# Scans with a constant of their own, small operations on other engines, and a fixed order of the score matmuls

## The chip, the cores and the metric

The kernel runs on one core of one Trainium2 chip. The metric is the time of one execution in device microseconds, as the median of several runs. In the profile PE is TensorE (PEld its weight loads), DVE is VectorE, ACT is ScalarE, POOL is GpSimd and SP is SyncE, which here only issues DMAs.

## The reference

Three layers follow each other. The first is a gated linear attention over 4 batches, 8 heads, 768 steps and 48 dimensions:

```
for t in range(S):
    state = alpha[t][:, None] * state + outer(k[t], v[t])
    y[t] = q[t] @ state
```

Its output, 3072 tokens by 384, is normalised (RMS) and goes through a gated layer, `silu(x @ w_gate) * (x @ w_val) @ w_out`, with an inner width of 1536. The last layer is a mixture of 8 experts: each token goes to the expert with the largest logit, `relu(x @ w1[e]) @ w2[e]` (inner width 1024), and the result is scaled by two gates. All is float32.

## The kernel before

The attention is cut into 24 tiles of 128 steps (6 per batch). Three tiles make a group of 384 tokens, and there are 8 groups. Tiles 0 to 2 are the first tiles of three batches; in the order of tiles a state is therefore needed again three tiles later.

For one tile, the decay `alpha` is transposed (`al`, 128 partitions by 4 pairs of heads by 128 steps). For tiles 0 to 4 PE transposes it and the scans read PSUM; for tiles 5 and 6 PE transposes and ACT copies to SBUF; from tile 7 on DVE transposes from SBUF. `after_scan` (L310) then runs a scan backwards over the steps: it keeps the first column of `al` in `en`, sets that column to 0, sets the columns `begin[:, 1:, 0]` to 1, scans with `begin` as the added operand and multiplies `en` by the first column of the result, which gives the decay of the state over the whole tile. `upto_scan` (L324) writes reciprocals into `begin[:, :, 0]` and scans forwards with the same `begin`. `k` is multiplied with the one scan and `q` with the other (L351, L411).

`stages` (L415) holds what is done with a tile: `score` multiplies keys by queries on PE (L430), 8 matmuls for 4 pairs of heads and two halves `hh` (partitions 0 to 47 and 64 to 111), into one PSUM bank for each half; each float32 matmul is two records in the trace. Its `post` decays the state by `en` (L434, DVE) and masks the two score banks (L440, DVE). `outp` forms the outputs (L464, L468), whose sum of squares goes through two small POOL operations (L475, L476); `state` adds the tile's own part to the state; `xtr` transposes the result into `xh` and `xl`, the high and low float32r parts.

The gated layer needs weights in two float32r parts as well. They are made while it runs: DVE puts the words of a chunk together (L576, L579, L582), ACT rounds the high part (L595, L622), and DVE subtracts for the low part (L586). For a step j, PE computes `ps_g` and `ps_v` in 9 matmuls each (L650) and `ps_o` in 9 (L684); ACT and DVE turn the first two into `hh` and `hl` (L642, L661, L664, L670). `runs` gives the order: group 0 and group 1 with the steps 0 to 5, then both with the steps 6 to 11, then groups 2 to 7. `m_evac` (L689) copies the three `ps_o` banks after each run. While the first four runs go on, the tiles 3 to 8 of the attention are worked in between; from group 2 on, `strict` fixes the order of PE's instructions as written.

Tokens are scattered by expert into a table in DRAM (`route_b`, POOL's indirect DMAs, L769), which is first filled from a constant row, `zrow`, by way of the tile `zero` (L1010, SP's DMAs, L774). The experts follow, and behind them a branch (`overflow`, L1378) for tokens beyond the slots.

Each engine has one queue and works in order. What order that is, a planner decides when the kernel is built: it simulates the engines and issues on each the instruction that is ready, by order of writing among several. `tc.keep_in_program_order` ties an instruction behind the one written just before it on its engine; `pace` (L223) does so for the kinds listed for a stage, `seq` (L215) where `strict` is set.

```
seq(nc.tensor.matmul(ps[hh][:, p, :], lhsT=kT[r, p, :], rhs=qT[r, p, :], start=True, stop=True))
```

Of the kernel before, what the change touches and what calls it, by code (L numbers as in the profile page):

```python
# [8 lines left out]
F32 = mybir.dt.float32  # L9
# [3 lines left out]
AF = mybir.ActivationFunctionType  # L13
ALU = mybir.AluOpType
# [41 lines left out]
def gla_glu_moe_kernel(  # L56
# [16 lines left out]
    nc = tc.nc  # L73
    P = 128
    B, H, S, D = q.shape
    NT, DM = out.shape
    NP = H // 2
# [8 lines left out]
    GT = 3  # L86
# [4 lines left out]
    RW = DM + 2  # L91
# [7 lines left out]
    FAR = float(1 << 20)  # L99

    const = ctx.enter_context(tc.tile_pool(name="const", bufs=1, side="right"))
# [9 lines left out]
                            base=0, pattern=[[-1, P]], channel_multiplier=1)  # L111
# [3 lines left out]
                            base=0, pattern=[[1, P]], channel_multiplier=-1)  # L115
# [8 lines left out]
                   allow_small_or_imprecise_dtypes=True)  # L124
    tokid = const.tile([P, NTILE, 1], F32, name="tokid")
    nc.gpsimd.iota(tokid[:, 0:NTILE - NCH, 0], pattern=[[P, NCH], [S, B - 1]], base=0, channel_multiplier=1,
                   allow_small_or_imprecise_dtypes=True)
    nc.gpsimd.iota(tokid[:, NTILE - NCH:, 0], pattern=[[P, NCH]], base=S * (B - 1), channel_multiplier=1,
                   allow_small_or_imprecise_dtypes=True)
# [6 lines left out]
                   allow_small_or_imprecise_dtypes=True)  # L136
    rank_at = const.tile([P, E, 1], F32, name="rank_at")
    for r0_, a0_, a1_ in RANKS:
        nc.gpsimd.iota(rank_at[:, a0_:a1_, 0], pattern=[[1, a1_ - a0_]], base=r0_, channel_multiplier=0,
                       allow_small_or_imprecise_dtypes=True)  # L140
# [4 lines left out]
    for i, c in enumerate((REG, DM, F2)):  # L145
# [1 line left out]
    capE = const.tile([P, E, 1], F32, name="capE")  # L147
    gT = const.tile([P, KD], F32, name="gT")
    wr = const.tile([P, KD, RX], F32, name="wr")
    zrow = const.tile([P, 1, RW], F32, name="zrow")  # L150
    nc.gpsimd.memset(zrow, 0.0)
    nc.gpsimd.iota(zrow[:, 0, RW - 1:RW], pattern=[[0, 1]], base=int(FAR), channel_multiplier=1,
                   allow_small_or_imprecise_dtypes=True)


    wpool = tc.alloc_tile_pool(name="wpool", bufs=1, side="left")
# [1 line left out]
    att = tc.alloc_tile_pool(name="att", bufs=1, side="right")  # L158
# [40 lines left out]
    for i in range(1):  # L199
        t_ = att.tile([P, NP, 2 * D], F32, name=f"wide{i}")  # L200
        nc.gpsimd.memset(t_, 0.0)
        wide.append(t_)

    begin = att.tile([P, NP, P], F32, name="begin")
    nc.gpsimd.memset(begin, 0.0)

    vt = {}
    pre = {}
# [4 lines left out]
    strict = [False]  # L213

    def seq(ins):  # L215

        if strict[0]:
            tc.keep_in_program_order(ins)
# [4 lines left out]
    def pace(kind, ins):  # L223

        if kind in paced[0] or kind.rstrip('0123456789') in paced[0]:
            tc.keep_in_program_order(ins)
# [4 lines left out]
    def bank(shape, name):  # L231

        seat[0] += 1
        k_ = SEATS[seat[0] - 1] if spread[0] and seat[0] <= len(SEATS) else seat[0] % 7
        if spread[0] and k_ >= 3:
            return psM.tile(shape, F32, tag=("g", "v", "o0", "o1", "o2")[k_ - 3], name=name)
        return psA.tile(shape, F32, tag="att", name=name)
# [53 lines left out]
    def seat_of(t, nm, shape, bufs=1):  # L291
        if (t, nm) in SIDE:
            tag, i = SIDE[t, nm]
            if tag not in side:
                side[tag] = wpool.tile([P, 3, NP * P], F32, tag=tag, name="side")
            flat = side[tag][:, i, 0:shape[1] * (shape[2] if len(shape) > 2 else 1)]
            return flat.rearrange("p (a b) -> p a b", a=shape[1]) if len(shape) > 2 else flat
        return att.tile(shape, F32, tag=nm, name=nm, bufs=bufs)
# [8 lines left out]
    def flat(x):  # L307
        return x.rearrange("p a b -> p (a b)")

    def after_scan(Z, al):  # L310

        en = att.tile([P, NP, 1], F32, tag="en", name="en", bufs=4)
        W = NP * P
        k_ = 'sc' + str(now[0])
        pace(k_, nc.vector.tensor_copy(en, al[:, :, 0:1]))
        pace(k_, nc.vector.memset(al[:, :, 0:1], 0.0))
        pace(k_, nc.vector.memset(begin[:, 1:, 0:1], 1.0))
        pace(k_, nc.vector.tensor_tensor_scan(out=flat(Z)[:, W - 2::-1], data0=flat(al)[:, W - 1:0:-1],
                                              data1=flat(begin)[:, W - 1:0:-1], initial=1.0,
                                              op0=ALU.mult, op1=ALU.add))  # L320
        pace(k_, nc.vector.tensor_tensor(out=en, in0=en, in1=Z[:, :, 0:1], op=ALU.mult))
        return en

    def upto_scan(A, Z, al):  # L324
# [90 lines left out]
    def stages(t):  # L415
        b, c = place_of[t]
        first, final = c == 0, c == NCH - 1
        en, qT, kT = pre[t]
# [6 lines left out]
        def score():  # L425
            ps = [bank([P, NP, P], "ps_s") for _ in range(2)]
            for p in range(NP):
                for hh in range(2):
                    r = slice(64 * hh, 64 * hh + D)
                    seq(nc.tensor.matmul(ps[hh][:, p, :], lhsT=kT[r, p, :], rhs=qT[r, p, :], start=True, stop=True))  # L430

            def post():
                if not first:
                    nc.vector.tensor_tensor(out=Sc, in0=Sc, in1=en.to_broadcast([P, NP, D]), op=ALU.mult)  # L434
                    for hh in range(2):
                        nc.scalar.activation(S_[rs[hh], :, hh * D:hh * D + D], Sc[rs[hh]], AF.Copy)
                mb = mask.to_broadcast([P, NP, P])
                for hh in range(2):
                    Ph = seat_of(t, f"P{hh}", [P, NP, P])
                    pace(f'Ph{t}', nc.vector.tensor_tensor(out=Ph, in0=ps[hh], in1=mb, op=ALU.mult))  # L440
                    Pt[hh] = Ph
            return post
# [246 lines left out]
    def m_evac(s):  # L689
        g, j0, _ = runs[s]  # L690
        if not j0:
            rows[g] = act.tile([P, GT, WO], F32, tag="R", name="R")
        R = rows[g]
        for i in range(GT):
            if j0:
                nc.vector.tensor_tensor(out=R[:, i, :], in0=R[:, i, :], in1=obank[s][i], op=ALU.add)
            elif i == 1:
                nc.vector.tensor_copy(R[:, i, :], obank[s][i])
            else:
                nc.scalar.activation(R[:, i, :], obank[s][i], AF.Copy)  # L700
        del obank[s]
# [99 lines left out]
    def late_step():  # L801

        if late:
            job = late[0]
            got = job.pop(0)(*carry)
            carry[:] = [] if got is None else [got]
            if not job:
                late.pop(0)
                nconv[1] += 1
# [9 lines left out]
    def prep_step():  # L819
        if prep:  # L820
            prep.pop(0)()

    def slot(s, n):

        g, j0, _ = runs[s]
        j, what = j0 + n // 3, n % 3
        if what == 0:
            have(3 * j + 1, 0)
            return m_gate(g, j)
        if what == 1:  # L830
            have(3 * j + 2, 0)
            return m_val(g, j)
        m_low(g, j)
        if j > j0:
            have(3 * j, j)
            m_out(s, j - 1)
        elif s:
            have(3 * runs[s - 1][2], runs[s - 1][2])
            m_out(s - 1, runs[s - 1][2] - 1)
            return lambda: m_evac(s - 1)  # L840
# [27 lines left out]
    for do in START.split():  # L868
        what, t = do[0], int(do[1:] or 0)
# [108 lines left out]
    for s in range(4):  # L978
        strict[0] = s >= CFG['STRICT']
        N = 3 * (runs[s][2] - runs[s][1])  # L980
        paced[0] = CFG['K2'] if s else CFG['K1']
        for n in range(N):
            if (s, n) == (1, CFG['PREP6']):
                prep.extend(prework(nprep))
                nprep += 1
            late_step()
            post = slot(s, n)
            post2 = []
            while due(s, n):
                post2.append(stage())  # L990
                if s:
                    break
            for i in range(CFG['CR'][s]):
                conv_step()
                if i < CFG['PRN'][s]:
                    prep_step()
                if i == 1 and post:
                    post()
                    post = None
            if post:  # L1000
                post()
            for x in post2:
                if x:
                    x()
            if s == 0 and done % NST == 0:
                while prep:
                    prep_step()
            if s == 3 and n == 0:
                zero = act.tile([P, 1, RW], F32, tag="cF", name="zero", bufs=3)
                nc.scalar.activation(zero, zrow, AF.Copy)  # L1010
            if s == 3 and n < 2 * E and n % 2 == 0:
                init_bucket(n // 2)

# [364 lines left out]
    def overflow():  # L1378
        xp.release()
        op_ = tc.alloc_tile_pool(name="op", bufs=1, side="right", reuse_waits="tile")  # L1380
        with tc.If(nblk > 0):
            with tc.For_i(0, nblk, 1):
                def sm(nm, w=1, dt=F32):
                    return op_.tile([P, w], dt, tag=nm, name=nm)
# [57 lines left out]
                for j in range(KF2):  # L1442
                    ph = psE.tile([P, P], F32, tag="h", name="ph", bufs=2)
                    for i in range(KD):
                        nc.tensor.matmul(ph, lhsT=wa[:, i, j * P:j * P + P], rhs=xo[:, i, :],
                                         start=(i == 0), stop=(i == KD - 1))
# [46 lines left out]
    for u in range(U):  # L1493
        for j in range(KF2):
# [28 lines left out]
            if u > 1 and j == 3:  # L1523
                _, _, r, n = parts[u]
# [22 lines left out]
        if u == 1:  # L1547
            while ready or pw:
                weight_step()
            load_next(2)  # L1550
            fetch()
    op_ = overflow()
    u = U - 1
    for i in range(parts[u][3]):
# [40 lines left out]
```

## Time and profile before

| | |
|---|---|
| median of 3 runs | 820.66 us (820.44 to 821.23) |
| the profiled execution | 820.86 us, of which the span 819.0 us |
| busy, share of the span | PE 98%, PEld 94%, DVE 69%, ACT 40%, POOL 11% |
| granted TensorE clock | 0.997 over the span |

A busy time is the union of an engine's instructions. A matmul's record lasts longer than the time after which the next may start, so a busy PE can still lose time; that is read from the starts of matmuls that follow each other. In a timeline row, `x8` is a merged run of 8 instructions, and the second number is the time from the first's start to the last's end.

### The profile page before, as it was taken

The page shows a single profiled execution, that of the slowest core. Times are in us where ns is not written, and L with a number is a line of the kernel's source. Part 1 is how long each engine was busy: PE and PEld are TensorE (multiplying, and loading weights), DVE is VectorE, ACT ScalarE, POOL GpSimd, SP SyncE. Part 2 cuts the span into 40 slices and gives each one's busy share as a digit, 9 for nine tenths or more (in the row PEclk, how much of TensorE's full clock was granted, in tenths as well). Part 3 has the DMA queues.
Part 4 walks back from the last instruction along what each step waited for, and adds up shares of the span by engine and source line. Part 5 has one row for each costly group of instructions (what it writes and reads, how often), then busy time and mean ns, then how long its engine had stood idle before and what let it go on. Part 6 is the DMA issues. An engine that isn't in the chain of part 4 may idle for free.

```text
span 819.0 us, 15897 instructions
## 1 busy us (share of the span) xinstructions
PE 802.6 (98%) x5967; PEld 771.7 (94%) x5967; DVE 561.4 (69%) x1234; ACT 326.5 (40%) x694; POOL 91.3 (11%) x175
## 2 busy tenths in 40 slices
PE   7999999999999999999999999999999999999996
PEld 5899999999999999999999999999988999999996
DVE  7998999498677876767767662345358667677641
ACT  1756554333333333332433332225226455554441
POOL 3001000000300020010020011010021002211121
PEclk9999999999999999999999999999999999999998
DMA  9955575753543453344444221005047686688710
GB/s 200 215 142 153 160 163 167 214 142 95 146 111 92 113 130 76 83 112 96 102 115 102 47 46 44 20 21 183 1 142 209 169 223 186 214 245 251 204 54 28
DMA packets 195454, 106.85 MB, mean 130 GB/s; under 512 B 125868, under 2 KB 190122, under 8 KB 195376
## 3 DMA queue, kind: packets, MB, share of 16 engines
q1 hardware_dynamic: 190912, 96.35, 46.2%
q0 software_dynamic: 4464, 9.48, 3.5%
q8 instruction: 47, 0.77, 0.4%
q14 instruction: 31, 0.25, 0.1%
HBM read 80.88 MB, written 25.18 MB: 129 GB/s over the span
## 4 chain that ended last, share of the span: by engine, by line
PE 93%; issue 2%; DVE 2%; POOL 1%; ACT 1%; DMA 0%; POOLq 0%; DVEq 0%
PE ps_o L684 19%; PE ps_v L650 19%; PE ps_g L650 19%; PE ps_h L650 12%; PE ps_b L1205 8%; PE ps_s L430 3%; PE ps_b L1211 3%; PE ps_y L468 3%; PE ps_y L464 2%; PE ps_st L489 1%; PE pc L615 1%; PE ps_k L450 1%; PE ps_n L283 1%; DMA er<-bucket 0%; PE pt L607 0%
## 5 line engine op out<-in xcount | busy, mean ns | idle before, releaser
L664 ACT ACTIVATE hh<-tt 128x384 fp32r<-128x384 f32 x96 | 50.3, 524 | 143.2 <-DVE tt L661 133.2
L661 DVE TENSOR_TENSOR tt<-tt,ps_v 128x384 f32<-128x384 f32 x96 | 52.7, 549 | 77.8 <-PE ps_v L650 65.7
L642 ACT ACTIVATE tt<-ps_g 128x384 f32<-128x384 f32 x96 | 47.0, 490 | 86.1 <-PE ps_g L650 80.3
L670 DVE TENSOR_TENSOR hl<-tt,hh 128x384 fp32r<-128x384 f32 x96 | 52.9, 551 | 24.6 <-ACT hh L664 23.0
L1185 DVE SCALAR_TENSOR_TENSOR h<-ps_h,h 128x256 fp32r<-128x256 f32 (+6 forms) x72 | 38.1, 531 | 45.2 <-ACT h L1184 42.5
L684 PE MATMUL ps_o<-wol,hh 128*128 128x400 f32 x192 | 66.3, 346 | 0.0
L684 PE MATMUL ps_o<-woh,hh 128*128 128x400 f32 x192 | 65.2, 348 | 0.0
L1184 ACT ACTIVATE h<-ps_h 128x256 fp32r<-128x256 f32 (+6 forms) x72 | 33.5, 468 | 77.4 <-PE ps_h L650 76.5
L684 PE MATMUL ps_o<-woh,hl 128*128 128x400 f32 x192 | 63.7, 344 | 0.0
L650 PE MATMUL ps_h<-x,w1b 128*128 128x456 f32 (+3 forms) x288 | 57.2, 341 | 0.3 <-DVE h L1185 0.3
L650 PEld LDWEIGHTS ps_h<-x,w1b 128*128 128x128 f32 x288 | 50.6, 188 | 1.9 <-DVE h L1185 0.6
L650 PE MATMUL ps_h<-x,w1a 128*128 128x256 f32 (+3 forms) x288 | 52.2, 325 | 0.0
L650 PEld LDWEIGHTS ps_h<-x,w1a 128*128 128x128 f32 x288 | 47.3, 188 | 0.9 <-ACT x L1165 0.3
L650 PE MATMUL ps_g<-xh,wgh 128*128 128x384 f32 x192 | 46.1, 348 | 0.0
L440 DVE TENSOR_TENSOR P<-ps_s,mask 128x512 f32<-128x512 f32 x46 | 30.1, 685 | 23.0 <-PE ps_s L430 22.8
L650 PE MATMUL ps_v<-xh,wvh 128*128 128x384 f32 x192 | 45.8, 346 | 0.0
L650 PE MATMUL ps_v<-xl,wvh 128*128 128x384 f32 x192 | 44.1, 337 | 0.0
L1205 PE MATMUL ps_b<-h,w2b 128*128 128x456 f32 (+2 forms) x216 | 43.5, 343 | 0.5 <-issue 0.5
L650 PE MATMUL ps_g<-xh,wgl 128*128 128x384 f32 x192 | 44.0, 336 | 0.0
L650 PE MATMUL ps_g<-xl,wgh 128*128 128x384 f32 x192 | 43.8, 337 | 0.0
L650 PE MATMUL ps_v<-xh,wvl 128*128 128x384 f32 x192 | 43.8, 336 | 0.0
L1205 PEld LDWEIGHTS ps_b<-h,w2b 128*128 128x128 f32 x216 | 37.9, 188 | 2.2 <-issue 0.9
(312 smaller groups left out, 1880.3 us busy)
## 6 DMA issues: line engine op xcount, KB each, us to landing
st<-in_moe_w_dram SPq DMA_DIRECT2D x46, 384.0 KB
bucket<-zero SPq DMA_DIRECT2D x8, 772.0 KB
stg<-in_moe_w_gate_dram SPq DMA_DIRECT2D x12, 384.0 KB
stg<-in_moe_w_val_dram SPq DMA_DIRECT2D x12, 384.0 KB
stg<-in_moe_w_out_dram SPq DMA_DIRECT2D x12, 384.0 KB
v<-in_v_dram SPq DMA_DIRECT2D x23, 192.0 KB
more<-in_moe_w_dram SPq DMA_DIRECT2D x9, 384.0 KB
er<-in_moe_w_dram SPq DMA_DIRECT2D x9, 384.0 KB
```

Of the source, the lines that this page charges most:

```text
L430: seq(nc.tensor.matmul(ps[hh][:, p, :], lhsT=kT[r, p, :], rhs=qT[r, p, :], start=True, stop=True))
L440: pace(f'Ph{t}', nc.vector.tensor_tensor(out=Ph, in0=ps[hh], in1=mb, op=ALU.mult))
L468: seq(nc.tensor.matmul(ps[u, h * D:h * D + D], lhsT=Pt[h % 2][:, h // 2, u], rhs=vt[t][:, h, :], start=first, stop=True, skip_group_check= ...
L642: nc.scalar.activation(tt, ps, AF.Silu)
L650: seq(nc.tensor.matmul(ps, lhsT=a_[:, kc, :], rhs=b_[:, kc, :], start=(n == 0), stop=(n == 3 * KD - 1)))
L661: nc.vector.tensor_tensor(out=tt, in0=tt, in1=ps, op=ALU.mult)
L664: nc.scalar.activation(hh, tt, AF.Copy)
L670: nc.vector.tensor_tensor(out=hl, in0=tt, in1=f(hh), op=ALU.subtract)
L684: seq(nc.tensor.matmul(obank[s][i], lhsT=a_[:, sl], rhs=weight(b_, j), start=(j == j0 and n == 0), stop=(j == j1 - 1 and n == 2)))
L1184: nc.scalar.activation(hh[:, 0, :], ps, AF.Relu)
L1185: nc.vector.scalar_tensor_tensor(out=hh[:, 1, :], in0=ps, scalar=0.0, in1=f(hh[:, 0, :]), op0=ALU.max, op1=ALU.subtract)
L1205: nc.tensor.matmul(ob2[u][k_][:, 0:r * n], lhsT=we[p][b_][:, j, k_ * P:k_ * P + P], rhs=hh[:, a_, :], start=(j == 0 and m == 0), stop=(j = ...
```

## The change

The reverse scan gets a constant of its own, `ends` (0, with 1 in the first column of pairs 1 to 3), set once on POOL; the memset of `begin[:, 1:, 0:1]` before each reverse scan is gone. In `after_scan` the copy of `al`'s first column into `en` goes from DVE to ACT, and the product of `en` and `Z` from DVE to POOL; neither is paced any longer. In `score`, for tiles after tile 3, each matmul but the first of a tile is tied behind the one written before it, so that the two halves alternate (`strict` has all of them tied, as before). In `m_evac` the copy of the middle bank goes to ACT for the runs 0 and 1. The constant row `zrow` is no longer kept from the start: POOL writes `zero` itself, and the overflow branch makes its own.

```diff
-    zrow = const.tile([P, 1, RW], F32, name="zrow")
-    nc.gpsimd.memset(zrow, 0.0)
-    nc.gpsimd.iota(zrow[:, 0, RW - 1:RW], pattern=[[0, 1]], base=int(FAR), channel_multiplier=1,
-                   allow_small_or_imprecise_dtypes=True)
+
+    def empty(row):
+        nc.gpsimd.memset(row, 0.0)
+        nc.gpsimd.iota(row[:, 0, RW - 1:RW], pattern=[[0, 1]], base=int(FAR), channel_multiplier=1,
+                       allow_small_or_imprecise_dtypes=True)
...
-    begin = att.tile([P, NP, P], F32, name="begin")
-    nc.gpsimd.memset(begin, 0.0)
+    begin, ends = (att.tile([P, NP, P], F32, name=nm) for nm in ("begin", "ends"))
+    for t_ in (begin, ends):
+        nc.gpsimd.memset(t_, 0.0)
+    nc.gpsimd.memset(ends[:, 1:, 0:1], 1.0)
...
-        pace(k_, nc.vector.tensor_copy(en, al[:, :, 0:1]))
+        nc.scalar.activation(en, al[:, :, 0:1], AF.Copy)
         pace(k_, nc.vector.memset(al[:, :, 0:1], 0.0))
-        pace(k_, nc.vector.memset(begin[:, 1:, 0:1], 1.0))
         pace(k_, nc.vector.tensor_tensor_scan(out=flat(Z)[:, W - 2::-1], data0=flat(al)[:, W - 1:0:-1],
-                                              data1=flat(begin)[:, W - 1:0:-1], initial=1.0,
+                                              data1=flat(ends)[:, W - 1:0:-1], initial=1.0,
                                               op0=ALU.mult, op1=ALU.add))
-        pace(k_, nc.vector.tensor_tensor(out=en, in0=en, in1=Z[:, :, 0:1], op=ALU.mult))
+        nc.gpsimd.tensor_tensor(out=en, in0=en, in1=Z[:, :, 0:1], op=ALU.mult)
...
-                    seq(nc.tensor.matmul(ps[hh][:, p, :], lhsT=kT[r, p, :], rhs=qT[r, p, :], start=True, stop=True))
+                    ins = nc.tensor.matmul(ps[hh][:, p, :], lhsT=kT[r, p, :], rhs=qT[r, p, :], start=True, stop=True)
+                    if strict[0] or (t > GT and (p or hh)):
+                        tc.keep_in_program_order(ins)
...
-            elif i == 1:
+            elif i == 1 and s > 1:
                 nc.vector.tensor_copy(R[:, i, :], obank[s][i])
...
-                nc.scalar.activation(zero, zrow, AF.Copy)
+                empty(zero)
...
+        zrow = op_.tile([P, 1, RW], F32, name="zrow")
         with tc.If(nblk > 0):
+            empty(zrow)
```

## Rows read from the trace of the kernel before

**Rows 1.** The page's chain of work that ended last, by engine.

```profile
PE 93%; issue 2%; DVE 2%; POOL 1%; ACT 1%; DMA 0%; POOLq 0%; DVEq 0%
```

**Rows 2.** Waits of PE: line waited for, us in total, times, longest.

```profile
PE ps_n L283 <- POOL nat L270: 4.4, 1, 4.4
```

**Rows 3.** Stretches: length, busy us (instructions) of PE, PEld, DVE, ACT, POOL; clock, DMA.

```profile
5.00:20.00 15.00, 13.96 (x121) 10.49 (x119) 14.23 (x33) 1.28 (x4) 2.18 (x13) 1.00 1.31 227
...
35.00:50.00 15.00, 15.00 (x143) 14.48 (x142) 15.00 (x37) 7.73 (x16) 0.74 (x2) 1.00 0.58 169
50.00:75.00 25.00, 25.00 (x252) 22.75 (x250) 22.58 (x51) 14.48 (x36) 1.15 (x3) 1.00 0.59 156
```

**Rows 4.** Timeline of PE around tile 4's score matmuls: start, us, instruction.

```profile
51.47 1.16 PE L430 MATMUL ps_s<-qT,kT 48*128 48x128 f32 x8
52.55 0.78 PE L650 MATMUL ps_g<-xh,wgh 128*128 128x384 f32 x3
...
54.31 1.16 PE L430 MATMUL ps_s<-qT,kT 48*128 48x128 f32 x8
55.40 0.81 PE L684 MATMUL ps_o<-woh,hh 128*128 128x400 f32 x3
```

**Rows 5.** The same around tile 6's score matmuls.

```profile
130.90 1.16 PE L430 MATMUL ps_s<-qT,kT 48*128 48x128 f32 x16
132.00 0.79 PE L650 MATMUL ps_v<-xh,wvhe 128*128 128x384 f32 x3
```

**Rows 6.** The same around tile 7's score matmuls.

```profile
143.99 0.49 PE L430 MATMUL ps_s<-qT,kT 48*128 48x128 f32 x4
144.41 0.80 PE L650 MATMUL ps_g<-xh,wghe 128*128 128x384 f32 x3
...
146.18 0.94 PE L430 MATMUL ps_s<-qT,kT 48*128 48x128 f32 x12
147.05 0.61 PE L650 MATMUL ps_v<-xh,wvhe 128*128 128x384 f32 x2
```

**Rows 7.** Timeline of DVE at tile 0's reverse scan.

```profile
5.54 0.16 DVE L315 COPY en<-ps_n 128x4 f32<-128x4 f32 x1 [3.04 <-PE ps_n L283]
...
5.93 1.22 DVE L318 TENSOR_TENSOR_SCAN aT<-ps_n,begin 128x511 f32<-128x511 f32 x1
```

**Rows 8.** Timeline of DVE at tile 5's product of en and its reader.

```profile
59.74 0.16 DVE L321 TENSOR_TENSOR en<-en,Z 128x4 f32<-128x4 f32 x1
...
60.35 0.35 DVE L434 TENSOR_TENSOR state<-state,en 128x192 f32<-128x192 f32 x1
```

**Rows 9.** Groups of ACT's instructions: busy us, mean ns, idle before.

```profile
L620 ACT ACTIVATE Fo<-pc 128x16 f32<-128x16 f32 x12 | 2.2, 180 | 6.8 <-PE pc L615 6.6
```

**Rows 10.** Waits of DVE: us in total, times, longest.

```profile
DVE hl L670 <- ACT hh L664: 23.0, 41, 0.8
```

**Rows 11.** Groups of DVE's instructions: busy us, mean ns, idle before.

```profile
L698 DVE COPY R<-ps_o 128x400 f32<-128x400 f32 x8 | 4.6, 571 | 2.5 <-PE ps_o L684 2.5
```

**Rows 12.** Groups of POOL's instructions.

```profile
L205 POOL MEMSET begin<- 128x512 f32 x1 | 0.5, 515 | 0.0
L151 POOL MEMSET zrow<- 128x386 f32 x1 | 0.4, 411 | 0.0
```

**Rows 13.** Lines L476 and L411: duration ns minimum/median/maximum, first and last start.

```profile
L476 POOL TENSOR_TENSOR ss<-ss,mhalf x24: 549/551/876, 18.8 to 509.8; 128x1 f32<-128x1 f32 x24
...
L411 DVE TENSOR_TENSOR qT<-qT,aT x19: 675/684/689, 62.8 to 486.5; 128x512 f32<-128x512 f32 x19
```

**Rows 14.** Timelines around 417.9 us, of POOL and of DVE.

```profile
417.93 0.74 POOL L475 TENSOR_SCALAR ss<-ss 128x1 f32<-128x1 f32 x1 [2.73 <-ACT xn L474]
...
417.94 0.68 DVE L411 TENSOR_TENSOR qT<-qT,aT 128x512 f32<-128x512 f32 x1
```

**Rows 15.** Timelines of DVE and PE: a low weight part and its first use.

```profile
61.75 0.53 DVE L586 TENSOR_TENSOR wgl<-F,wgh 128x384 fp32r<-128x384 f32 x1
...
63.97 0.69 PE L650 MATMUL ps_g<-xh,wgl 128*128 128x384 f32 x3
```

## The prediction, made before the kernel was run

> **What bounds the kernel now.** I read the page's chain first: 93% of what ended last is PE's own work [rows 1], so a change that lightens another engine is worth nothing unless PE waits for that engine. The waits of PE come next: the one that stands out is at the very start, 4.4 us until POOL has set the padding of `nat` [rows 2]. The busy times by stretch say who is close behind PE. Up to 20 us DVE is the fuller one; from 35 to 50 us PE and DVE are both busy for all of it, from 50 to 75 us PE for all and DVE for 22.58 of 25.00 us [rows 3]. There the weights are converted on DVE just ahead of PE: a low part that is finished at 61.75 + 0.53 = 62.28 us is read at 63.97 us, 1.7 us later [rows 15]. So there are two places to win time: the first 20 us, where PE waits on a chain through DVE, and PE's own instructions.
>
> PE's own loss is seen in its timeline. Tile 4's score matmuls run as two blocks of 8 records, one for each half; from a block's start to the next instruction's they take 52.55 - 51.47 = 1.08 us and 55.40 - 54.31 = 1.09 us, 2.17 us in all [rows 4]. Tile 6 does the same 16 records in one block, in 132.00 - 130.90 = 1.10 us [rows 5]. Alternating halves cost PE half as much as one half after the other. Tile 5 repeats the pattern of tile 4, with blocks at 66.06 and 67.86 us; tile 7 is cut into 4 and 12 records and takes 0.42 + 0.87 = 1.29 us [rows 6]; tiles 3, 6 and all from 8 on are whole. Tiles 0 and 1 are split as well, but the new tie holds only for tiles after tile 3.
>
> **The change part by part.**
>
> The tie of the score matmuls. It adds no instruction. If tiles 4 and 5 each come out as one block, each saves 2.17 - 1.10 = 1.07 us. If the first matmul of a tile, which stays free, runs ahead of the rest, the cost is that of tile 7's cut, 1.29 us, and the saving 0.88 us. I take 1.0 us each, 2.0 us, and 0.15 us for tile 7 (between nothing and 0.19 us). Bounds: 1.76 to 2.33 us. What it takes away: half 0 can no longer be masked on DVE before half 1 is multiplied; but the second block's end, after which both can be masked, does not move back. A tied matmul that waits for its bank holds up whatever the planner put behind it in PE's queue; that would show as idle PE.
>
> The reverse scan. At tile 0, from the start of the copy to the start of the scan, DVE takes 5.93 - 5.54 = 0.39 us [rows 7] for the copy and two memsets, of which the memset of `al`'s column, 0.06 us, stays. The product is busy for 0.16 us [rows 8], about half of it beside the next instruction. That is at most 0.33 + 0.16 = 0.49 us a tile off DVE. The new copy on ACT is not in the trace; the nearest row is ACT's copy of 128x16 from PSUM, 180 ns [rows 9]. DVE must now wait for it before it sets the column to 0. What such a round trip costs is shown by `hl`, which waits for ACT's `hh`: 23.0 us over 41 waits, 0.56 us in the mean and 0.8 us at most [rows 10], most of it the 128x384 operation itself. At tile 0 DVE has nothing else to do, and ACT's 0.18 us and the hand-over take the place of the copy and the memset: I put that at nothing, and the product at 0.08 us. At tiles 1 and 2 DVE has other work, and ACT is busy for 1.28 of the 15 us [rows 3], so about 0.25 us each is won: 0.5 us over three tiles, rounded down. Bounds: 3 x 0.49 = 1.5 us won, and 3 x (0.8 + 0.06 - 0.39 - 0.08) = 1.2 us lost.
>
> Against it stands POOL's start. The memset of `ends` is as large as that of `begin`, 515 ns, and that of `zrow`, 411 ns, is gone from before it [rows 12]; with the small memset of the column this is some 0.15 us more before POOL sets `nat`, for which PE's first transposes wait [rows 2]. The beginning is worth 0.5 - 0.15 = 0.35 us; I take 0.3 us.
>
> From tile 3 on, up to 140 us, DVE loses some 0.25 us of work at each of six tiles, and in the evacuations of runs 0 and 1 two copies of 571 ns [rows 11], about 2.6 us by then. PE is the bound there, so none of it counts by itself; it is the cover for the tie: PE will ask for its weights some 2.5 us earlier, and they are made 1.7 us ahead of use [rows 15]. With that lead alone 0.8 us of the gain would be lost. ACT takes the two copies beside work that fills 14.48 of 25 us [rows 3].
>
> The product on POOL. The nearest row is L476, a tensor_tensor of 549 to 876 ns [rows 13]; I take 0.55 us. It costs nothing as long as L434, which reads `en`, comes later: at tile 5 L434 starts 0.6 us after the product did [rows 8], and POOL could start at the scan's end. Behind the product in POOL's queue stand the norm's two operations, whose result PE needs microseconds later. Bounds: 0 to 0.3 us (876 ns less the 0.6 us) at tiles 5 to 8, where PE has other matmuls.
>
> What such an operation meets is in the trace: POOL's L475 took 0.74 us at 417.93 us, when DVE's L411 began 0.01 us behind it, and that L411 took 0.68 us [rows 14], as all of its line do, 675 to 689 ns [rows 13]. POOL waits there, and DVE does not. The Trainium skill (SBUF — State Buffer, section "Who interferes with whom") says that a VectorE instruction with two inputs in SBUF and a GpSimd one that reads SBUF exclude each other, and that the one that starts first blocks the other. The trace agrees that they exclude each other, but not on who waits.
>
> `zero` from POOL in place of ACT, and the constant in the branch: nothing, as POOL is busy for about a microsecond in 25 [rows 3]; if POOL came late, SP's queue would hold the fill of the table and the loads behind it, for 0.4 us by the memset of `zrow` [rows 12].
>
> The sum: 2.15 us for PE and 0.3 us for the beginning, 2.45 us, off the profiled execution's own 820.86 us: 818.4 us. That execution (span 819.0 us and 1.9 us around it) lies 0.2 us above the median of 820.66 us, so the median should be 818.2 us.
>
> **The rivals.**
>
> The weights bind. PE gains in its own work, but stands still until DVE has converted. For it: DVE is full from 35 to 50 us [rows 3]. Against: 1.7 us of lead and DVE's own relief add up to more than 2.45 us. If other weights come closer than the one shown, only DVE's relief up to tile 5 is won, 0.5 us and three times 0.25 us less POOL's 0.15 us, 1.1 us: 819.6 us.
>
> The product holds DVE. If POOL's operation did block the forward scan behind it, DVE would give back 4 x 0.55 = 2.2 us at tiles 5 to 8, nearly all its relief; the lead of 1.7 us would be left for the tie, and with the beginning 2.0 us would be won at the most, 1.1 us if the weights bind too: 819.1 us between them. Against: the row of L411. This is what the named page's rule would do here.
>
> The tie does not join the halves. The planner may put other matmuls between the tied ones, or PE may wait for the second bank as long as it saves. For it: the blocks of tile 4 are 54.31 - 52.55 = 1.8 us apart [rows 4], so the second bank may have been late. Against: tiles 6 and 8 are whole without a tie. Then only the beginning is left, 0.3 us: 820.4 us.
>
> DVE waits for ACT. The column can't be set to 0 before ACT has copied it, and ACT works in order. If the copy stands behind one larger operation at each scan, the way to the scan takes 0.8 + 0.06 us [rows 10] in place of 0.39 us. At the first three scans that is 1.2 us net on the chain to PE's first real matmuls, 1.35 us with POOL's start; at tiles 3 to 6 it is 4 x 0.47 = 1.9 us more, above the lead of the weights, so that the tie's gain goes into waiting, and some 0.6 us of it beyond: 820.66 + 1.95 = 822.6 us. It decides from about 0.7 us per scan on. For it: from 50 us on ACT is busy for more than half [rows 3]. Against: the planner can put other DVE work ahead of the memset, and at first ACT is nearly empty.
>
> **How the numbers follow.** A measurement of this kernel tells about 0.2%, 1.6 us, from no change: faster is below 819.0 us, slower above 822.3 us. The forecast has 0.55 (0.06 of it above 819.0 us), weights that bind 0.14 (a third below), the product 0.04 (half below), the tie that does not join 0.14, DVE waiting for ACT 0.13, nearly all of it above 822.3 us. So faster has 0.57, same 0.30, slower 0.13. With both ends of its terms the forecast's own range is 816.8 to 820.2 us: 2.33 us and 1.5 - 0.15 us won at the low end, rounded down for switches between kinds of matmul that I leave out; 1.76 us won and 1.35 us lost at the high end. The range to hold 8 in 10 goes on over the other cases into the last one: 816.7 to 821.9 us.
>
> **What would show it right or wrong.** Right: tiles 4 and 5 show their 16 records of L430 in 1.1 to 1.3 us; PE's first L650 starts some 0.3 us sooner, and by 150 us PE is at the same matmul some 2.5 us sooner; that distance stays to the end; no wait of PE over half a microsecond is new between 35 and 150 us. Wrong: waits of DVE at L316 for ACT above 0.5 us at several tiles; waits of PE for weights made at L586; L430 still in blocks of 8; L434 waiting for POOL with `ps_y` late behind it.

## The result, and the profile after

After the change the median is 827.93 us (827.70 to 832.54 over five runs), against 820.66 us before (820.18 to 821.23): a ratio of 1.0098, with an interval from 1.0081 to 1.0116. The kernel is 7.3 us slower; forecast were 818.2 us and a range that ended at 821.9 us. All five runs count in the ratio, the two above 829 us too, which had a mean granted clock of 0.989 and 0.988 for 0.996 in the others. The profiled execution took 827.93 us, with a span of 826.1 us.

The page of the changed kernel, busy times and the chain by engine:

```profile
PE 809.1 (98%) x5967; PEld 777.8 (94%) x5967; DVE 555.4 (67%) x1160; ACT 330.5 (40%) x719; POOL 101.1 (12%) x201
...
PE 92%; issue 2%; DVE 2%; POOL 1%; ACT 1%; DMA 0%; POOLq 0%; DVEq 0%; ACTq 0%
```

PE's share of the chain is 92% for 93% [rows 1]; nothing in this view says where the 7.3 us went. The answer comes from setting the same matmul of the two traces side by side. PE's first `ps_g` matmul starts 3.05 us late (38.08 us for 35.03 us). At 144 us the distance is 3.05 us again, and from there it grows in a straight line to 7.1 us at 571 us; behind the experts it is 7.4 us. So there are two losses: one within the first 35 us, and a drift in a stretch in which PE waits for nothing. The first and last start of one group of 150 matmuls shows both (first before, then after):

```profile
L650 PE MATMUL ps_g<-xh,wgh x150: 332/338/447, 158.3 to 566.6; 128*128 128x384 f32 x150
```

```profile
L654 PE MATMUL ps_g<-xh,wgh x150: 335/338/445, 161.7 to 573.7; 128*128 128x384 f32 x150
```

408.3 us between them before, 412.0 us after. Start to start, the `ps_g` and `ps_v` matmuls take 176.5 and 176.7 ns in the mean for 173.2 and 173.3 ns before; those of `ps_o` take 182.5 ns in both. What became slower is the matmuls that read `xh` and `xl`, and the change does not touch them. It touches where they lie: the 1544 bytes of `zrow` left the constants, and every tile behind them moved. In the layout of the built programs `xh` begins at byte 185,792 of a partition before and at 187,360 after: 64 bytes past a multiple of 128, and then 96.

The first loss is seen on POOL. Timeline of the changed kernel, POOL, then DVE in the same stretch, then ACT (start, us, instruction; idle time ahead of it in brackets):

```profile
22.67 2.38 POOL L479 TENSOR_SCALAR ss<-ss 128x1 f32<-128x1 f32 x1 [3.77 <-ACT side L478]
25.14 0.56 POOL L480 TENSOR_TENSOR ss<-ss,mhalf 128x1 f32<-128x1 f32 x1
```

```profile
22.31 0.55 DVE L586 SCALAR_TENSOR_TENSOR F<-stg,F 128x384 int32<-128x384 int32 x1
22.78 0.55 DVE L583 SCALAR_TENSOR_TENSOR Fo<-stg,Fo 128x384 int32<-128x384 int32 x1
23.25 0.35 DVE L580 TENSOR_SCALAR F<-stg 128x384 int32<-128x384 int32 x1
23.52 0.55 DVE L586 SCALAR_TENSOR_TENSOR Fo<-stg,Fo 128x384 int32<-128x384 int32 x1
23.99 0.55 DVE L590 TENSOR_TENSOR wvl<-F,wvh 128x384 fp32r<-128x384 f32 x1
24.46 0.55 DVE L583 SCALAR_TENSOR_TENSOR F<-stg,F 128x384 int32<-128x384 int32 x1
24.93 1.28 DVE L444 TENSOR_TENSOR P<-ps_s,mask 128x512 f32<-128x512 f32 x2
```

```profile
25.73 0.58 ACT L481 ACTIVATE side<-ps_y,ss 128x384 f32<-128x384 f32 x1 [2.31 <-POOL ss L480]
```

The norm's mean of tile 1, one number per partition, takes 2.38 us. It ends at 25.05 us, with the last of DVE's overlapping instructions that read SBUF alone (24.46 + 0.55 = 25.01 us), just after DVE has gone over to products that read PSUM. Before, the same instruction took 0.39 us:

```profile
22.98 0.39 POOL L475 TENSOR_SCALAR ss<-ss 128x1 f32<-128x1 f32 x1 [3.30 <-ACT side L474]
```

DVE's order there is another one than before; the planner lays it out anew with every edit. PE's longest waits from 20 to 35 us follow, before and then after, and then its stretches after (us, PE busy, granted clock, DMA share, GB/s):

```profile
PE ps_x L539 <- ACT xn L477: 0.5, 1, 0.5
```

```profile
PE ps_x L543 <- ACT side L481: 1.8, 1, 1.8
```

```profile
20.00:25.00 5.00, 4.35 (x49) 1.00 0.93 154
25.00:30.00 5.00, 3.63 (x28) 0.75 1.45 184
30.00:35.00 5.00, 4.85 (x69) 0.91 1.04 284
```

The wait is 1.3 us longer. After it the granted clock falls, part of the time to the lower level of 1.2 GHz: 0.75 and 0.91 in two stretches that had 1.00 before. That is worth at most 5 x 0.25 + 5 x 0.09 = 1.7 us. With the 1.3 us it makes at most 3.0 us of the 3.05 us seen at 35 us, in this one execution; how often other executions meet a lower clock there comes up below.

The tie itself did what it says. Score matmuls of tiles 4, 5 and 7 after (compare [rows 4, 6]):

```profile
54.70 1.16 PE L432 MATMUL ps_s<-qT,kT 48*128 48x128 f32 x16
...
69.38 0.48 PE L432 MATMUL ps_s<-qT,kT 48*128 48x128 f32 x2
...
70.51 1.16 PE L432 MATMUL ps_s<-qT,kT 48*128 48x128 f32 x14
...
147.05 0.48 PE L432 MATMUL ps_s<-qT,kT 48*128 48x128 f32 x2
...
149.24 1.16 PE L432 MATMUL ps_s<-qT,kT 48*128 48x128 f32 x14
```

Tile 4 is whole, and tiles 5 and 7 are cut in 2 and 14. The distance to the kernel before falls from 3.05 to 2.02 us at 63 us; by 93 us it is 2.83 us again. Two waits of PE stand between, which the kernel before does not have from 35 to 150 us: one for the norm by way of ACT, one for a weight part made on DVE.

```profile
PE ps_x L543 <- ACT xn L481: 0.5, 1, 0.5
PE ps_g L654 <- DVE wgl L590: 0.4, 1, 0.4
```

### The profile page after: what moved, and what is told of

The parts are those of the page before. It is cut to its first block, busy times and chain, and to the rows that moved or that the text cites. A ratio compares the mean times of both kernels' runs of the same rounds, so it can differ in the third digit from the quotient of the medians.

```text
span 826.1 us, 15911 instructions
## 1 busy us (share of the span) xinstructions
PE 809.1 (98%) x5967; PEld 777.8 (94%) x5967; DVE 555.4 (67%) x1160; ACT 330.5 (40%) x719; POOL 101.1 (12%) x201
## 4 chain that ended last, share of the span: by engine, by line
PE 92%; issue 2%; DVE 2%; POOL 1%; ACT 1%; DMA 0%; POOLq 0%; DVEq 0%; ACTq 0%
PE ps_o L688 19%; PE ps_v L654 19%; PE ps_g L654 19%; PE ps_h L654 12%; PE ps_b L1209 8%; PE ps_s L432 3%; PE ps_b L1215 3%; PE ps_y L472 3%; PE ps_y L468 2%; PE ps_st L493 1%; PE pc L619 1%; PE ps_k L454 0%; PE pt L611 0%; PE ps_n L286 0%; PE ps_x L543 0%
```

## Experiments: the places in SBUF

Theory: matmuls that read `xh` and `xl` from 96 bytes past a multiple of 128 are slower. Rival: the drift is a consequence of the other order.

**32 bytes more in front of them**, in the changed kernel (`e1`) and in the kernel before (`e2`), and 64 bytes in the kernel before (`e3`). No engine gets another instruction.

```diff
-    gT = const.tile([P, KD], F32, name="gT")
+    gT = const.tile([P, KD + 8], F32, name="gT")[:, 0:KD]
```

> The changed kernel with one constant tile 32 bytes longer, so that the activations behind it lie 32 bytes lower; the order of instructions on every engine is the same. Theory (placement): without the constant row the activations xh and xl moved by 1568 bytes, from a multiple of 64 bytes to 32 past one, and each of the 1728 matmuls that stream 384 columns of them takes 176 to 177 ns in place of 173; with the 32 bytes it is 173 ns again, and the time falls by 4 us or a little more, to about 823.8 us. Rival (the loss after 140 us comes from the new work on ScalarE and GpSimd, or from another order): nothing changes, 827.9 us.

> The kernel before with the same tile 32 bytes longer; same order on every engine. Theory (placement): xh and xl now start 32 past a multiple of 64 bytes, L650 on them takes 176 to 177 ns, and the time rises by about 4.5 to 5 us, to 825.3 us. Rival: 820.7 us, unchanged.

> The kernel before with that tile 64 bytes longer; same order on every engine. If it is the remainder to 64 bytes that counts: 820.7 us, unchanged, L650 at 173 ns. If any move of these tiles counts, or the remainder to 128 bytes: about 825 us.

`e1` (64 bytes past): 823.5 us for 821.97 us of the kernel before on the same chip, ratio 1.0021 (1.0010 to 1.0033). The drift is gone, and the distance stays at 2.78 us from 287 to 571 us:

```profile
L654 PE MATMUL ps_g<-xh,wgh x150: 332/338/448, 161.3 to 569.4; 128*128 128x384 f32 x150
```

408.1 us, as before the change (408.3 us). The 2.38 us of POOL stay. The medians are 1.5 us apart and not 2.78: the profiled execution, 825.25 us, was one of the slower of the twelve (822.15 to 825.98 us), and behind the gated layer it lost 2.1 us more, with a granted clock of 0.67 from 615 to 620 us. In that stretch `e2` and `e3` had 0.70 and 0.66. `e2` (32 past): ratio 1.0028 (1.0016 to 1.0040), 409.8 us for the same group, so 1.5 us of drift; that is less than the 4.5 to 5 us that I had expected. `e3` (0 past): ratio 1.0006 (0.9993 to 1.0020), and 408.7 us for the group. So place alone makes 7.1 - 2.78 = 4.3 us of the 7.3 us by the traces, without any change of order; by the medians of the two comparisons it is 7.3 - 1.5 = 5.8 us.

**The matmul by itself** (`e4`, `e5`): series of 36 matmuls of 384 fp32r columns, moving operand and weights at shifted offsets.

In outline:

```python
for nm, mo, wo in (("m0", 0, 0), ("m32", 8, 0), ("m64", 16, 0), ("m96", 24, 0), ("w32", 0, 8), ("w64", 0, 16)):
    series(ps, mo, wo, 36)   # matmul(ps, lhsT=wt[:, wo + ...], rhs=mov[:, mo:mo + 384])
```

> Not the kernel: a probe of the two suspected costs by themselves. It computes nothing of the reference. Part 1: six series of 36 matmuls of 384 columns, moving operand at 0, 32, 64 and 96 bytes past a multiple of 64, then the weights at 32 and 64. Placement theory: about 173 ns from start to start at 0 and 64, 176 to 177 ns at 32 and 96; no difference for the weights. Part 2: GpSimd's tensor_scalar of 128x1 is released while VectorE runs 8 tensor_tensors back to back, the first 1, 2, 4 or 8 of them with two inputs in SBUF and the rest with one. Theory (starved GpSimd): it ends only when the run of two-input ones ends, so about 0.6, 1.1, 2.0 and 3.9 us; with none it takes 0.2 us; VectorE's own durations stay at 0.55 us. Rival (turns are taken): never above 0.8 us, and VectorE loses time in its place.

Start to start, the moving operand costs 173.3 ns at 0, 32 and 64 bytes past a multiple of 128 and 176.7 ns at 96; in the second probe 173.3 at 0 and 32, 175.0 at 80, 176.7 at 96 and 173.4 at 112. Shifted weights cost 173.7 ns at 32, 174.7 at 64 and 173.3 at 96. I had expected a loss at 32 bytes too, and none for the weights. The 3.4 ns of the 96 are, within 0.1 ns, the 3.3 ns of the changed kernel, and 936 such matmuls between 288 and 571 us times 3.3 ns are 3.1 us, where its distance grew from 4.26 to 7.10 us, by 2.8 us. The slower half of `e2` is not explained by this: 32 bytes past cost nothing here, and 0.7 to 1.0 ns there. Nor is `e3`: at 0 past its `ps_g` matmuls took 1.1 ns more than before and its `ps_o` matmuls 1.0 ns less.

## Experiments: the first 35 us

Theory: DVE's unbroken run holds POOL's mean, and by ACT the transposes of tile 1. Rival: the start is late by the new order itself, and the long mean is only a sign of it.

**The run broken by a wait** (`e8`). The changed kernel with one copy more on DVE, which must wait for POOL's result; its own 4 bytes take 32 and bring `xh` back to 64 past.

```diff
+    mean1 = const.tile([P, 1], F32, name="mean1")
...
+                if t == 1:
+                    nc.vector.tensor_copy(mean1, ss)
```

> The changed kernel with one more VectorE copy of 128x1 that waits for GpSimd's mean and power of tile 1, planned behind the integer step of the run that blocked it (the copy's own 4 bytes bring xh and xl back to 64 past a multiple of 128). Theory (the unbroken run of VectorE holds GpSimd from 22.67 to 25.05 us): VectorE stops at about 23.5 us, GpSimd's mean ends at about 23.6 and its power at 24.3 us, ScalarE's scaling of tile 1 starts 1.2 us earlier than in the changed kernel, and the time is 1.0 to 1.4 us below that kernel with the 32 bytes (ratio to before about 1.0005 instead of 1.0021). Rival (the start is late for another reason, GpSimd's long operation is only a sign of it): VectorE loses 0.9 us more, the scaling starts no earlier, and the ratio is 1.002 to 1.0035.

POOL, DVE and ACT of this kernel:

```profile
22.65 0.98 POOL L480 TENSOR_SCALAR ss<-ss 128x1 f32<-128x1 f32 x1 [3.77 <-ACT side L479]
23.71 0.56 POOL L481 TENSOR_TENSOR ss<-ss,mhalf 128x1 f32<-128x1 f32 x1
```

```profile
23.23 0.35 DVE L583 TENSOR_SCALAR F<-stg 128x384 int32<-128x384 int32 x1
24.30 0.15 DVE L483 COPY mean<-ss 128x1 f32<-128x1 f32 x1 [0.72 <-POOL ss L481]
```

```profile
24.30 0.58 ACT L484 ACTIVATE side<-ps_y,ss 128x384 f32<-128x384 f32 x1 [0.91 <-POOL ss L481]
```

DVE stands still for 0.72 us, and in that time POOL ends, 0.05 us behind DVE's last instruction (23.58 us). ACT's scaling starts 1.43 us sooner, the clock stays at 1.00 up to 35 us, and the first `ps_g` is 0.66 us late in place of 3.28 us in `e1`. At 571 us the distance to the kernel before is 0.07 us in place of 2.78 us. So the added wait ended the hold, and these two executions are 2.7 us apart in PE's time, twice the 1.0 to 1.4 us that I expected.

How much of that belongs to the hold is not shown, as the clock of an execution is not the order's alone. In `e3`, whose order at the start is that of the kernel before, the first `ps_g` was 1.62 us late without any new wait, with this stretch:

```profile
20.00:25.00 5.00, 4.26 (x41) 0.66 1.00 167
```

`e10`, whose start is that of the kernel before too, had 0.67 there and was 1.58 us late. Over all runs `e8` has the ratio 1.0006 (0.9988 to 1.0024) and `e1` 1.0021 (1.0010 to 1.0033): 1.2 us, as expected, but the intervals overlap. And `e8` met a lower clock too: six of its twelve runs took 820.3 to 820.9 us at a mean clock of 0.997 to 0.999, the other six 823.7 to 825.6 us at 0.990 or 0.991.

**Without the scan part** (`e7`, and the same kernel again as `e12`): tie, output copies and the freed row as in the change, the scans as before, 32 bytes.

```diff
-    begin, ends = (att.tile([P, NP, P], F32, name=nm) for nm in ("begin", "ends"))
+    begin = att.tile([P, NP, P], F32, name="begin")
...
-        nc.scalar.activation(en, al[:, :, 0:1], AF.Copy)
+        pace(k_, nc.vector.tensor_copy(en, al[:, :, 0:1]))
...
-        nc.gpsimd.tensor_tensor(out=en, in0=en, in1=Z[:, :, 0:1], op=ALU.mult)
+        pace(k_, nc.vector.tensor_tensor(out=en, in0=en, in1=Z[:, :, 0:1], op=ALU.mult))
```

> The changed kernel without its scan part (copies, products and the marks around the scans as before, one constant), with tie, output copies and the freed row of zeros, and 32 bytes that bring xh and xl back to 64 past a multiple of 128. Theory (the 3 us at the start come from the scan part, by the order on VectorE that it brings): GpSimd's mean of tile 1 takes under 1 us, TensorE's first gate matmul starts within 0.6 us of before, and the ratio is 0.9976 to 1.0005. Rival (they come from another part, or any new order on VectorE blocks GpSimd as well): the mean takes 2 us or more, the first gate matmul is 2 to 3 us late and the ratio is 1.002 or more.

> The same kernel as the one without the scan part (tie, output copies, the freed row, 32 bytes). Its profiled execution stood 2.55 us behind the kernel before from 150 us on, with a granted clock of 0.50 from 15 to 25 us, while the median of its runs was 1.9 us below. Theory (the clock of that execution was chance; the kernel itself gains by the tie): with the clock at 1.00 up to 35 us TensorE is 0.5 to 1.5 us earlier than before at 150 us, and the ratio is 0.9975 to 0.9995. Rival (its order at the start brings the lower clock): again 0.5 to 0.8 somewhere before 25 us, TensorE 2 us late at 150 us, and the ratio 1.000 or more.

The mean of tile 1 takes 0.48 us in the one and 0.53 us in the other: without the scan part it is not held for long. The first profile was still 2.55 us late, with half the clock from 15 to 25 us; the second was not. Stretches of the two (PE, PEld, DVE, ACT and POOL busy, then the granted clock):

```profile
15.00:20.00 5.00, 5.00 (x46) 4.36 (x46) 4.24 (x11) 1.57 (x4) 0.76 (x2) 0.50 1.11 283
20.00:25.00 5.00, 5.00 (x44) 3.76 (x44) 4.42 (x10) 1.62 (x5) 0.00 (x0) 0.50 0.89 167
```

```profile
15.00:20.00 5.00, 4.86 (x77) 4.11 (x76) 5.00 (x13) 1.79 (x5) 0.77 (x2) 1.00 1.11 293
20.00:25.00 5.00, 4.13 (x48) 2.99 (x47) 5.00 (x12) 3.68 (x11) 1.08 (x2) 1.00 0.91 165
```

With the clock at 1.00 the first `ps_g` is 0.50 us early, where `e8` still has it 0.66 us late, and PE is 0.55 us ahead of the kernel before at 144 us and 0.40 us ahead at 571 us. The 0.66 us of `e8` stay unexplained. The times do not settle it: ratios of 0.9988 (0.9973 to 1.0003) and 1.0009 (0.9992 to 1.0026). In `e12` seven runs took 820.4 to 822.6 us at a mean clock of 0.996 to 0.998, and five 825.5 to 825.8 us at 0.989 or 0.990; the 17 runs of the kernel before beside it lay between 821.2 and 824.5 us, and none was below 0.994. So this kernel meets a lower clock in part of its runs, where only the profiled execution of `e7` shows that it was at the start, and my word of chance was half wrong. Nor is that its order's alone: two of the twelve runs of `e6` below, whose scans are those of the kernel before, had a mean clock of 0.990 as well.

**POOL beside DVE by itself** (`e5`, `e9`, `e11`): POOL's 128x1 operation released inside runs of overlapping DVE instructions. In outline:

```python
nc.gpsimd.tensor_scalar(out=s[i], in0=x[:, n - 1:n], scalar1=0.5, scalar2=1e-6, op0=ALU.mult, op1=ALU.add)
for f in what:   # 1 to 8 products; or L586, L583, L580, L586, L590, L583 in the changed kernel's order, twice
    f()
```

> Computes nothing of the reference; only its own rows count. VectorE runs 1, 2, 4 or 8 products with two SBUF inputs, this time each into its own output so that they overlap as the conversions in the changed kernel do at 22.3 to 24.9 us; GpSimd's 128x1 operation is released just as the run begins. Theory (an unbroken run of such products holds GpSimd to its end): the small operation takes about 0.55, 1.0, 1.95 and 3.8 us beside 1, 2, 4 and 8 of them, and about 0.19 us beside eight products that read PSUM and SBUF. Rival (it waits for one product, whatever follows): 0.5 to 0.6 us in all four. With one one-input operation as third of the run (two products, it, five products), the theory by the row of the kernel before at 22.98 us says it gets through there (about 1.1 us), by the row of the changed kernel at 22.67 us that it does not (about 3.6 us). TensorE: 384 columns at 0, 32, 96, 80 and 112 bytes past a multiple of 128: 173.3, 173.3, 176.7 at 96 as the first probe had it, 80 and 112 not known, at most 176.7 and at least 173.3.

> Computes nothing of the reference; only its own rows count. GpSimd's 128x1 operation is released by ScalarE at four moments (operations of 1, 64, 128 and 256 columns) inside runs of ten or twelve VectorE instructions that overlap: plain products into outputs of their own, products in place, the integer steps and low parts in the very order of the run that met GpSimd in the changed kernel, and the integer steps with two inputs alone. First theory (what holds GpSimd is the moment of its request against the next instruction's start: it was 0.11 us ahead of one in the changed kernel, 0.28 us in the last probe): in every one of the four runs one or two of the moments give 1 us or more, the others at most 0.6 us. Second theory (it is the integer steps on pairs of words): plain and in-place products never above 0.6 us, the steps 1 us or more. Third theory (neither: it needs the other engines of the full kernel): at most 0.6 us in all sixteen.

> Computes nothing of the reference; only its own rows count. The run of integer steps and low parts from the changed kernel once more, with GpSimd's 128x1 operation released inside it at four moments: alone, beside loads into SBUF, beside ScalarE's copies, beside TensorE's matmuls, and beside all three. Theory (what the lone probe lacked is the other engines' traffic in SBUF): at most 0.6 us alone, and 1 us or more in at least one of the groups beside loads, copies or matmuls. Rival (it is something in the kernel that none of these is): at most 0.6 us in all twenty.

POOL in `e5` beside 2, 4 and 8 products from SBUF, then beside eight that read PSUM:

```profile
61.55 0.42 POOL L68 TENSOR_SCALAR s<-trig 128x1 f32<-128x1 f32 x1 [54.20 <-DVE trig L67]
63.43 0.42 POOL L68 TENSOR_SCALAR s<-trig 128x1 f32<-128x1 f32 x1 [1.46 <-DVE trig L67]
66.24 0.42 POOL L68 TENSOR_SCALAR s<-trig 128x1 f32<-128x1 f32 x1 [2.40 <-DVE trig L67]
70.93 0.19 POOL L68 TENSOR_SCALAR s<-trig 128x1 f32<-128x1 f32 x1 [4.27 <-DVE trig L67]
```

Beside one product it was 0.42 us too, and in `e4`, whose products all went into one output and so did not overlap, 0.54 us beside every run of products from SBUF. In `e9` and `e11` it took 0.26 to 0.58 us in all 36 cases, whatever the run, the moment, or the loads, copies and matmuls beside it. So my theory that an unbroken run holds POOL failed in every probe: there it was never held for longer than about one instruction of DVE. That DVE's run held it in the kernel is shown by `e8`, where POOL ended with DVE's stop, at 23.63 us and not at 25.05 us; which property of that run closes the gaps between its instructions stays open.

## Experiments: the tie and the output copies alone

**The tie in the kernel before** (`e6`), and with the output copies (`e10`):

```diff
-                    seq(nc.tensor.matmul(ps[hh][:, p, :], lhsT=kT[r, p, :], rhs=qT[r, p, :], start=True, stop=True))
+                    ins = nc.tensor.matmul(ps[hh][:, p, :], lhsT=kT[r, p, :], rhs=qT[r, p, :], start=True, stop=True)
+                    if strict[0] or (t > GT and (p or hh)):
+                        tc.keep_in_program_order(ins)
...
-            elif i == 1:
+            elif i == 1 and s > 1:
```

> The kernel before with the change's tie of the score matmuls alone; the order on VectorE in the first 35 us, the constants and the places in SBUF stay as before. Theory (the tie does what was forecast, and what made the changed kernel slow is the start and the places): tiles 4, 5 and 7 give their score blocks in one or two runs, the same matmul starts about 1.0 us earlier than before at 63 us, and the time is 0.5 to 2.0 us less than before (ratio 0.9976 to 0.9994). Rival (the gain is given back where the weights bind at 60 to 120 us, as the changed kernel's difference rose again from 2.02 at 63 us to 3.05 at 118 us): ratio 0.9995 to 1.0005. Second rival (the tie itself costs time): ratio above 1.001.

> The kernel before with the tie and with the output copies of the first two groups on ScalarE; nothing of the scans is changed. The tie alone won 0.75 us of TensorE's time, and its second half was lost because TensorE waited 0.4 us at 65.5 us for ScalarE's scaling behind GpSimd's mean. Theory (from 50 to 75 us the chain over ScalarE and GpSimd binds, not VectorE): two copies more on ScalarE win nothing, TensorE is at the same matmul 0.4 to 0.8 us earlier than in the kernel before at 150 us, ratio 0.9985 to 1.0002. Rival (VectorE's conversions bind, as the forecast of the changed kernel counted): VectorE is relieved of two times 0.57 us and TensorE is 1.2 us or more earlier at 150 us, ratio 0.9985 or less.

`e6`: ratio 0.9996 (0.9982 to 1.0011). PE is 0.68 us ahead after tile 4, 0.12 us at 65.6 us, and 0.75 us from tile 5 on, to the end of the gated layer; I had expected about 1.0 us. Each of the two tiles comes in 2 and 14 records, 0.41 + 1.08 = 1.49 us for 2.17 us, and wins 0.68 us; tile 7 stays at 4 and 12. What tile 4 won goes into a wait of PE, and behind it stands POOL once more. PE's only new wait from 35 to 150 us, and POOL:

```profile
PE ps_x L541 <- ACT xn L479: 0.4, 1, 0.4
```

```profile
63.12 1.06 POOL L477 TENSOR_SCALAR ss<-ss 128x1 f32<-128x1 f32 x1 [1.76 <-ACT xn L476]
64.26 0.55 POOL L478 TENSOR_TENSOR ss<-ss,mhalf 128x1 f32<-128x1 f32 x1
```

The mean of tile 4, 0.31 us in the kernel before, is held over two of DVE's products, `hl` at 62.98 us and `qT` at 63.44 us. `e10`: ratio 0.9988 (0.9976 to 1.0000); the wait of 0.4 us is the same, and from 36 to 144 us PE wins 0.77 us, as with the tie alone. The copies win nothing, as the theory had it. No kernel of these is shown to be faster than the kernel before: only `e10`'s interval ends at 1.0000, the others reach above it.

## Why the prediction was wrong, point by point

- **What bounds the kernel**: right. PE bounds it, and what made it slower is PE's own matmuls and one wait ahead of them.
- **"`zero` from POOL in place of ACT, and the constant in the branch: nothing."** This step failed, and it is the largest: I priced the instructions of the freed row and not its 1544 bytes. It moved `xh` and `xl` to 96 bytes past a multiple of 128, 3.3 ns for each matmul that reads them, 4.3 us in all (`e1`).
- **The product on POOL and what it meets**: right that POOL waits and DVE does not, wrong in what followed from it. I priced POOL's waiting for the product alone, at 0 to 0.3 us, with PE busy elsewhere, and called the norm's operations needed "microseconds later". At tile 1 the norm's mean is on the way to PE's next transposes. With the new order on DVE it was held for 2.38 us, and in the traces of single executions PE was 2.7 to 3 us late with it, up to 1.7 us of that through the clock; by the runs, ending the hold won 1.2 us, which the intervals do not separate from nothing. The product itself took 0.20 us in the median where I had taken 0.55 us. The Trainium skill (SBUF — State Buffer, section "Who interferes with whom") calls the port pair that the two engines share an exclusive lock and says that issue order decides who blocks. POOL's side of these rows fits a lock; the order does not fit, as POOL, at 22.67 us, waits on through five instructions that start after it.
- **The tie**, 2.15 us: mechanism right, size wrong. Alone it won 0.75 us, since tile 7 won nothing, the first matmuls ran ahead in tiles 4 and 5 (the case I had put at 0.88 us for a tile, 0.68 us measured), and 0.56 us went into the wait for the norm. In the changed kernel with the right places (`e1`) the distance fell by 0.5 us from 35 to 144 us; DVE's relief was no cover there, as PE waited 0.5 us for the norm and 0.6 us for `wgl`.
- **The beginning**, 0.3 us won: wrong in sign. The copy on ACT took 0.17 us, as estimated, and DVE cleared the column at 5.87 us, early. But the scan waited for the small memset of `ends`, which POOL issued last of its memsets, and started at 6.10 us for 5.93 us [rows 7]; the forward scan followed at 7.57 us for 7.48 us:

```profile
5.87 0.06 DVE L319 MEMSET ps_n<- 128x4 f32 x1 [3.38 <-ACT en L318]
6.10 1.22 DVE L320 TENSOR_TENSOR_SCAN aT<-ps_n,ends 128x511 f32<-128x511 f32 x1 [0.17 <-POOL ends L208]
```

```profile
5.97 0.09 POOL L208 MEMSET ends<- 128x3 f32 x1
```

- **The rivals**: the weights bound only for 0.4 us at one place (PE for `wgl`), and the tie joined the halves. DVE did wait for ACT ahead of clearing the column, above 0.5 us at five tiles after tile 0, but only once before 160 us (0.68 us at 31.02 us); the others, 0.70 to 1.45 us, came from 312 us on, where PE waited for nothing. Both causes of the 7.3 us were in none of the rivals.
- **What would show it wrong**: I had listed late products, waits for ACT and waits for weights. Some came: those of DVE for ACT, one of 1.0 us for a product at 297 us, one of PE for `wgl`; none of them explains the loss. The waits that counted were for the norm, and the largest loss showed as no wait at all.

## What to carry to other kernels

Before you price an edit at nothing, ask what it does to the addresses of everything allocated behind it, and compare start to start times of the busiest instruction: a few nanoseconds on a matmul that runs 1,728 times cost more here than all that the change was forecast to win. A small operation on GpSimd in a chain towards TensorE was held here through six instructions of VectorE, in an order that came with moving work off VectorE; one deliberate wait ended that, though the runs do not show that it paid. Set one execution beside another only with the granted clock of each stretch, and ask the medians whether they agree. Where a planner lays out the order, every edit is an edit of the whole neighbourhood, so look again at waits that were short before.

## What the runs showed of the hardware

- A 128x128 by 128x384 fp32r matmul at the upper clock took 173.3 ns from start to start with its moving operand 0, 32 or 64 bytes past a multiple of 128, 175.0 ns at 80, 176.7 ns at 96, and 173.4 ns at 112; in the kernel 173.2 to 173.4 ns at 64 and 176.5 to 176.7 ns at 96.
- A GpSimd operation of 0.19 us took up to 2.38 us behind six overlapping VectorE instructions, and 0.26 to 0.58 us inside runs of such instructions in probes.
- After a wait of 1.8 us TensorE's granted clock was 0.75 and 0.91 in the next two stretches of 5 us; in another kernel it was 0.50, the lower level, from 15 to 25 us, where one wait of 0.55 us, at 9.6 us, had gone before it since the first matmul; and with the start of the kernel before it was 0.66 and 0.67 from 20 to 25 us in two executions and 1.00 in three.
